# Attention ahead of two expert layers: exponentials transposed undivided, outputs multiplied by turned reciprocal sums

## The chip, the cores and the metric

The kernel runs on one core of a Trainium2 chip. [...] The metric is device time in microseconds; below are the median, the lowest and the highest of three runs.

## The reference

```python
def attention(q, k, v, M_prev, z_prev, beta):      # B, H, S, D = 4, 8, 576, 64
    scores = q @ k.T / 8, causal mask, minus the row's maximum
    a = np.exp(scores)
    a /= a.sum(-1, keepdims=True) + 1e-09
    local = a @ v
    q_p = phi(q)                                   # relu(x) + min(exp(x), 1)
    mem_out = (q_p @ M_prev) / (q_p @ z_prev + 1e-06)
    g = 1 / (1 + np.exp(-beta))                    # one per head
    return g * mem_out + (1 - g) * local

x = attention(...) as [2304, 512]
x = moe(x)      # gate by 8 rounds of row and column normalization; 8 experts 512 -> 1024 -> 512
return moe2(x)  # 512 -> 2048 -> 512, leaky relu
```

## The kernel before

Attention takes 32 heads in 16 pairs: a batch `b` and two neighbouring heads `j` = 0, 1. `run` (line 286) is a generator that emits the work of a pair and yields a number after each piece; what is emitted in between comes from outside. Up to the end of batch 0 the outside adds only the loading of weights. From then on, each yield adds one or two quarter steps of the first expert's products (`First.run`, tiles `ph`, `hh`, `hl`, `po`; 15 quarter steps in a pair). A planner then orders the instructions of each engine; where two are ready it keeps the order of emission. After the last pair come the gate, its normalization and the rest of the first expert, and from about 520 us on the other experts and the second layer, in an order written out by hand.

All products run on operands split in a high and a low part: ACT rounds the high part out of PSUM, DVE (or POOL) subtracts it from the source. So every transpose by PE (128x128 blocks against an identity) is followed by an ACT copy and a DVE subtraction.

A pair goes so. `load` (109) fetches q, k, v, M and z by DMA. `transposed` (127) turns q, k and, later, the features (`qT`, `kT`, `pT`; tile `tps`). `features` (158) makes phi(q) in place, multiplies by z, sums to `nrm`, and at line 177 POOL multiplies the features by g over the norm. For each head, `scores` (197) and `softmax` (208) work on five row blocks t: products into `sps`, a DVE instruction adds the mask and finds the maximum (214), an ACT exponential sums its row into `sm` (216). `normalize` (219) turns `sm` into (1 - g) over the sum and multiplies the blocks `a`: three on DVE (227), two on ACT (229). One head later, `turn` (235) transposes the blocks in three groups r, x, y into the `at_` tiles, of which there is one set. `outputs` (250) multiplies the turned features by M and the turned blocks by v, 18 products into one tile `avps`, and ACT copies half of it (270); `collect` (273) adds the other half on DVE (277). With the second head `collect` also rounds x to `xh` on DVE (280), stores x by DMA, and leaves `late`, by which POOL makes `xl` (282). `values` (179) splits v and M.

The head of index j is so emitted: scores and softmax of its blocks between the turns of the head before; `qT` of the next pair (j = 1); `outputs` of the head before, `normalize`, `collect` of the head before; then for j = 0 `values`, `late`, `pT`, `load` of the next pair, and for j = 1 `kT` and the first half of the features of the next pair. The tiles `sps`, `avps`, `tps` and the turned group y share the tag `big` in PSUM: three buffers in batch 0, two from then on.

Of the kernel before, what the change touches and what calls it, by code (L numbers as in the profile page):

```python
# [16 lines left out]
ALU = mybir.AluOpType  # L17
# [43 lines left out]
class Attention:  # L61
# [47 lines left out]
    def load(self, b, hp):  # L109
        nc, h0 = self.nc, 2 * hp  # L110
        r = {"b": b, "hp": hp}
        for nm, src in (("q", self.q), ("k", self.k), ("v", self.v)):
            t = self.nv if nm == "v" else self.sbt([P, 5, 2, D], "n" + nm)
# [44 lines left out]
    def features(self, r):  # L158
# [12 lines left out]
        nrm = self.sbt([P, 5, 2], "nrm")  # L171
# [4 lines left out]
        ph3 = ph.rearrange("p c h d -> p (c h) d")  # L176
        nc.gpsimd.tensor_mul(ph3, ph3, nrm.rearrange("p c h -> p (c h)").unsqueeze(2).to_broadcast([P, 10, D]))

# [14 lines left out]
    def head(self, r, j):  # L193
        sm, nm = self.sbt([P, 5], "sm", bufs=2), self.sbt([P, 5], "nm_", bufs=2)
        return {"r": r, "j": j, "a": {}, "sm": sm, "nm": nm}
# [23 lines left out]
    def normalize(self, s, t0, t1):  # L219
        nc, h = self.nc, 2 * s["r"]["hp"] + s["j"]  # L220
        sl = s["sm"][:, t0:t1]
        nc.vector.tensor_scalar(out=sl, in0=sl, scalar1=1e-9, scalar2=self.iomg[:, h:h + 1], op0=ALU.add, op1=ALU.mult)
        nc.vector.reciprocal(sl, sl)
        for t in range(t0, t1):
            a = s["a"][t]
            if t < 3:
                nc.vector.tensor_scalar(out=a, in0=a, scalar1=s["sm"][:, t:t + 1], scalar2=None, op0=ALU.mult)
            else:
                nc.scalar.activation(a, a, AF.Copy, scale=s["sm"][:, t:t + 1])  # L229
# [43 lines left out]
    def collect(self, s):  # L273
# [4 lines left out]
        if j == 1:  # L278
            hp, c0 = r["hp"], r["b"] * S
            nc.vector.tensor_copy(self.xh[:, hp, c0:c0 + S], r["x"])  # L280
# [5 lines left out]
    def run(self):  # L286
# [8 lines left out]
        for n in range(len(pairs)):  # L295
            last = n + 1 == len(pairs)
            for j in range(2):
                s = self.head(r, j)
                lo = self.turn(prev, "r") if prev is not None else None
# [28 lines left out]
                if j == 1 and not last:  # L328
                    self.transposed(nxt, "qT")
                if prev is not None:  # L330
                    self.outputs(prev)
                self.normalize(s, 0, 5)
                if prev is not None:
                    self.collect(prev)
                yield 4
                if j == 0:
                    self.values(r)
                    if prev is not None:
                        self.late()
                        if prev["r"]["hp"] == HP - 1:  # L340
                            yield ("done", prev["r"]["b"])
                    self.transposed(r, "pT")
                    if not last:
                        nxt = self.load(*pairs[n + 1])
                    yield 5
                elif not last:
# [831 lines left out]
```

## Time and profile before

| | |
|---|---|
| median of three runs | 2236.46 us (2235.49 to 2237.0) |
| profiled execution, first to last instruction | 2234.6 us |
| what the median has beyond that span | 1.9 us |
| PE busy | 2165.0 us (97%) |
| DVE busy | 1562.9 us (70%) |
| ACT busy | 870.0 us (39%) |
| POOL busy | 1108.8 us (50%) |
| attention, by the first and last rounding of x | 50.2 to 417.5 us |

Busy times are of the whole span, and their shares average over stages that have different limits. PE's durations overlap, since products are pipelined: a busy PE is not one at its peak.

### The profile page before, as it was taken

What the parts mean: (1) busy time and instruction counts of PE and PEld (TensorE: products, weight loads), DVE (VectorE), ACT (ScalarE), POOL (GpSimd) and SP (SyncE); (2) the same over time, 40 slices, a digit from 0 to 9 for tenths busy, and PEclk for the clock granted to TensorE, in tenths of its full rate; (3) what the DMA queues carried; (4) which work ended last, traced back from release to release, by engine and by line L of the source; (5) the groups of instructions that cost most, each with busy time, mean ns of one, the idle gap of its engine ahead of it and who ended that gap; (6) DMA issues with size and microseconds to landing.
All of it is one profiled execution on the core that took longest, in us unless ns stands there. A gap on an engine that the chain in (4) does not pass through costs nothing.

```text
span 2234.6 us, 36326 instructions
## 1 busy us (share of the span) xinstructions
PE 2165.0 (97%) x13973; PEld 1938.1 (87%) x13973; DVE 1562.9 (70%) x2904; ACT 870.0 (39%) x1753; POOL 1108.8 (50%) x993
## 2 busy tenths in 40 slices
PE   6799999989999999999999999999999999999999
PEld 5688889778888999998998988889898988898898
DVE  8989899565877777777777788855555554566565
ACT  7877777433332222223222233332333233332421
POOL 5132222244775455455444568854555543665550
PEclk9999999999999999999999999999999999999999
DMA  5233332224542222222124634421111152336111
GB/s 138 63 89 94 92 96 82 68 90 147 161 142 67 67 67 76 76 67 67 57 71 152 213 116 135 125 72 52 57 51 45 57 201 68 109 95 227 66 57 38
DMA packets 215757, 213.01 MB, mean 95 GB/s; under 512 B 71968, under 2 KB 169248, under 8 KB 214048
## 3 DMA queue, kind: packets, MB, share of 16 engines
q1 hardware_dynamic: 215584, 210.69, 30.4%
q8 instruction: 110, 1.80, 0.3%
q14 instruction: 63, 0.52, 0.1%
HBM read 157.83 MB, written 49.28 MB: 93 GB/s over the span
## 4 chain that ended last, share of the span: by engine, by line
PE 76%; DVE 9%; issue 5%; ACT 4%; POOL 4%; DMA 2%; SPq 0%; POOLq 0%; DVEq 0%; ACTq 0%
PE po L882 35%; PE pq L839 27%; PE pq L827 4%; PE ph L514 3%; PE po L522 2%; PE sps L206 2%; PE atps L245 1%; ACT a L229 1%; PE avps L261 1%; POOL stl L687 1%; DVE a L214 1%; ACT a L216 1%; DMA xa<-xd 1%; DVE x L277 1%; ACT x L270 0%
## 5 line engine op out<-in xcount | busy, mean ns | idle before, releaser
L882 PE MATMUL po<-w,hh 128*128 128x512 f32 x2592 | 810.6, 393 | 7.9 <-ACT acc L894 3.1
L882 PEld LDWEIGHTS po<-w,hh 128*128 128x128 f32 x2592 | 473.9, 188 | 106.2 <-DVE acc L892 3.3
L882 PE MATMUL po<-w,hl 128*128 128x512 f32 x1296 | 509.4, 393 | 0.0
L629 POOL TENSOR_TENSOR w0l<-raw,w0h 128x512 fp32r<-128x512 f32 x144 | 191.3, 1349 | 360.3 <-ACT w0h L628 360.3
L857 ACT ACTIVATE hh<-c 128x512 fp32r<-128x512 f32 x224 | 129.2, 624 | 476.0 <-DVE c L852 476.0
L882 PEld LDWEIGHTS po<-w,hl 128*128 128x128 f32 x1296 | 243.6, 188 | 56.1
L839 PE MATMUL pq<-Xh,w0h 128*128 128x256 f32 x960 | 266.2, 277 | 2.1 <-DVE uv L847 1.4
L839 PE MATMUL pq<-Xl,w0h 128*128 128x256 f32 x960 | 265.3, 276 | 0.0
L839 PE MATMUL pq<-Xh,w0l 128*128 128x256 f32 x960 | 265.1, 276 | 0.0
L858 DVE SCALAR_TENSOR_TENSOR hl<-c,hh 128x512 fp32r<-128x512 f32 x224 | 169.3, 797 | 79.3 <-ACT hh L857 79.3
L892 DVE SCALAR_TENSOR_TENSOR acc<-po,Pm,acc 128x512 f32<-128x512 f32 x252 | 178.4, 748 | 49.3 <-PE po L882 47.4
L629 POOL TENSOR_TENSOR w<-raw,w 128x512 fp32r<-128x512 f32 x144 | 199.8, 1405 | 1.7 <-ACT w L628 1.7
L847 DVE TENSOR_TENSOR uv<-pq,s 128x256 f32<-128x256 f32 x144 | 60.5, 420 | 191.8 <-ACT s L846 191.6
L839 PEld LDWEIGHTS pq<-Xh,w0h 128*128 128x128 f32 x960 | 180.1, 188 | 7.3 <-DVE uv L847 2.0
L839 PEld LDWEIGHTS pq<-Xl,w0h 128*128 128x128 f32 x960 | 180.2, 188 | 4.1
L839 PEld LDWEIGHTS pq<-Xh,w0l 128*128 128x128 f32 x960 | 180.2, 188 | 0.0
L846 ACT ACTIVATE s<-pq 128x256 f32<-128x256 f32 x144 | 54.9, 381 | 256.1 <-PE pq L839 256.0
L629 POOL TENSOR_TENSOR ql<-raw,qh 128x512 fp32r<-128x512 f32 x48 | 62.8, 1329 | 129.8 <-ACT qh L628 129.8
L861 ACT ACTIVATE hh<-c 128x512 fp32r<-128x512 f32 x64 | 40.5, 632 | 185.9 <-DVE c L860 185.9
L839 PE MATMUL pq<-Xh,w1h 128*128 128x256 f32 x384 | 106.1, 276 | 1.1 <-ACT xa L957 1.1
L839 PE MATMUL pq<-Xh,sh 128*128 128x256 f32 x384 | 106.0, 276 | 0.0
L839 PE MATMUL pq<-Xl,sh 128*128 128x256 f32 x384 | 106.0, 276 | 0.0
(325 smaller groups left out, 5557.4 us busy)
## 6 DMA issues: line engine op xcount, KB each, us to landing
raw<-in_moe_w_dram SPq DMA_DIRECT2D x136, 512.0 KB, 3.6
Xh<-kh SPq DMA_DIRECT2D x6, 1792.0 KB, 7.4
Xl<-kl SPq DMA_DIRECT2D x6, 1792.0 KB, 11.5
f<-in_moe_w_in_dram SPq DMA_DIRECT2D x16, 512.0 KB, 5.0
f<-in_moe_w_out_dram SPq DMA_DIRECT2D x16, 512.0 KB, 4.7
raw<-wide_in SPq DMA_DIRECT2D x16, 512.0 KB, 3.4
raw<-wide_out SPq DMA_DIRECT2D x16, 512.0 KB, 3.7
kh<-sth SPq DMA_DIRECT2D x12, 512.0 KB, 5.2
```

What stands on the lines that cost most here:

```text
L206: nc.tensor.matmul(ps[:, o_:o_ + kn], x[:, q0:q0 + P], y[:, k0:k0 + kn], start=(i == 0), stop=(i == len(terms) - 1))
L514: nc.tensor.matmul(ph[:, :T], wp[:, c, f0:f0 + P], x[:, c, t0:t0 + T], start=(n == 0), stop=(n == 11))
L522: nc.tensor.matmul(po, a[:, s], wp[:, c, :], start=(first and n == 0), stop=(last and n == 2))
L629: self.nc.gpsimd.tensor_sub(lo, src, f32(hi))
L827: nc.tensor.matmul(ph[:, f * SB:(f + 1) * SB], wp(a, c % 2), xp[x][:, c], start=(n == 0), stop=(n == 11))
L839: nc.tensor.matmul(b[-1][:, o:o + SB], wp(a, c), X[s][part][:, x, c], start=(n == 0), stop=(n == 5))
L846: nc.scalar.activation(s1, b[0][:, lo], AF.Copy)
L847: v.tensor_add(uv[:, 0], b[0][:, up], s1)
L857: nc.scalar.activation(hh[:, f], c, AF.Relu)
L858: v.scalar_tensor_tensor(out=hl[:, f], in0=c, scalar=0.0, in1=f32(hh[:, f]), op0=ALU.max, op1=ALU.subtract)
L882: nc.tensor.matmul(po[j], a[:, f, r], w[1, part][:, f], start=(fp == 0 and f == 0 and n == 0), stop=(fp == 1 and f == 1 and n == 2))
L892: nc.vector.scalar_tensor_tensor(out=acc[t], in0=po[j], scalar=Pm[:, t0 + t, e:e + 1], in1=acc[t], op0=ALU.mult, op1=ALU.add)
```

## The change

The exponentials are no longer divided. They are transposed as they are, and the output, which lies with the tokens along its columns, is multiplied at the end by a tile of reciprocal sums that has been turned in the same way. Since the features' part of the output is multiplied too, the features are first multiplied by the sums. The pair keeps both heads' sums in one tile `sm` of 5 by 2. The new `rows` (after the second head's softmax) makes sums / (1 - g), multiplies `nrm` by it, takes the reciprocals, has POOL multiply the features (the former line 177) and spread the reciprocals over 128 by 640. The new `spread` transposes that on PE into PSUM, and ACT copies it to `row`. `collect` has POOL multiply x by `row` and ACT, not DVE, round it. Since the features need both sums, `pT` moves to the end of the second head, and `outputs` of a pair's first head to the start of the next pair, ahead of the turns of the second head; those of the second head stay where they were, behind `spread`. q gets two buffers, and so does `nrm`. The last pair yields two more numbers.

```diff
-            t = self.nv if nm == "v" else self.sbt([P, 5, 2, D], "n" + nm)
+            t = self.nv if nm == "v" else self.sbt([P, 5, 2, D], "n" + nm, bufs=2 if nm == "q" else 1)
...
-        nrm = self.sbt([P, 5, 2], "nrm")
+        nrm = r["nrm"] = self.sbt([P, 5, 2], "nrm", bufs=2)
...
-        ph3 = ph.rearrange("p c h d -> p (c h) d")
+
+    def rows(self, r):
+
+        nc, h0 = self.nc, 2 * r["hp"]
+        sm, nrm = r["sm"], r["nrm"]
+        nc.vector.scalar_tensor_tensor(out=sm, in0=sm, scalar=1e-9, in1=self.iomg[:, h0:h0 + 2].unsqueeze(1).to_broadcast([P, 5, 2]),
+                                       op0=ALU.add, op1=ALU.mult)
+        nc.vector.tensor_mul(nrm, nrm, sm)
+        nc.vector.reciprocal(sm, sm)
+        ph3 = r["p"].rearrange("p c h d -> p (c h) d")
         nc.gpsimd.tensor_mul(ph3, ph3, nrm.rearrange("p c h -> p (c h)").unsqueeze(2).to_broadcast([P, 10, D]))
+        r["row"] = self.sbt([P, 5, 2, D], "rb")
+        nc.gpsimd.tensor_copy(r["row"].rearrange("p c h d -> p (c h) d"), sm.rearrange("p c h -> p (c h)").unsqueeze(2).to_broadcast([P, 10, D]))
...
-    def normalize(self, s, t0, t1):
-        nc, h = self.nc, 2 * s["r"]["hp"] + s["j"]
-        sl = s["sm"][:, t0:t1]
-        nc.vector.tensor_scalar(out=sl, in0=sl, scalar1=1e-9, scalar2=self.iomg[:, h:h + 1], op0=ALU.add, op1=ALU.mult)
-        nc.vector.reciprocal(sl, sl)
-        for t in range(t0, t1):
-            a = s["a"][t]
-            if t < 3:
-                nc.vector.tensor_scalar(out=a, in0=a, scalar1=s["sm"][:, t:t + 1], scalar2=None, op0=ALU.mult)
-            else:
-                nc.scalar.activation(a, a, AF.Copy, scale=s["sm"][:, t:t + 1])
+    def spread(self, r):
+
+        nc = self.nc
+        ps = self.big("rps")
+        for t in range(5):
+            q0 = 448 if t == 4 else t * P
+            nc.tensor.transpose(ps[:, P + q0:2 * P + q0], r["row"][:, t].rearrange("p h d -> p (h d)"), self.ident)
+        r["row"] = self.sbt([P, S], "row")
+        nc.scalar.activation(r["row"], ps[:, P:P + S], AF.Copy)
...
-            nc.vector.tensor_copy(self.xh[:, hp, c0:c0 + S], r["x"])
+            nc.gpsimd.tensor_mul(r["x"], r["x"], r["row"])
+            nc.scalar.activation(self.xh[:, hp, c0:c0 + S], r["x"], AF.Copy)
...
                 s = self.head(r, j)
+                if j == 0 and prev is not None:
+                    self.outputs(first)
+                    self.collect(first)
...
-                if j == 1 and not last:
-                    self.transposed(nxt, "qT")
-                if prev is not None:
+                if j == 1:
+                    self.rows(r)
+                    if not last:
+                        self.transposed(nxt, "qT")
+                elif prev is not None:
+                    self.spread(prev["r"])
                     self.outputs(prev)
-                self.normalize(s, 0, 5)
-                if prev is not None:
                     self.collect(prev)
...
-                    self.transposed(r, "pT")
+                    if not last:
+                        nxt = self.load(*pairs[n + 1])
+                    first = s
+                    yield 5
+                else:
                     if not last:
-                        nxt = self.load(*pairs[n + 1])
-                    yield 5
-                elif not last:
-                    self.transposed(nxt, "kT")
-                    yield 5
-                    f = self.features(nxt)
-                    next(f)
+                        self.transposed(nxt, "kT")
+                    yield 5
+                    self.transposed(r, "pT")
+                    if not last:
+                        f = self.features(nxt)
+                        next(f)
                     yield 6
...
+        self.outputs(first)
+        self.collect(first)
         for nm in "rxy":
             self.turn(prev, nm)()
             yield 7
+        self.spread(prev["r"])
         self.outputs(prev)
```

## Rows read from the trace of the kernel before

**Rows 1.** The page, busy time of each engine, share of the span, instructions:

```profile
PE 2165.0 (97%) x13973; PEld 1938.1 (87%) x13973; DVE 1562.9 (70%) x2904; ACT 870.0 (39%) x1753; POOL 1108.8 (50%) x993
```

**Rows 2.** Two lines' instructions: count, least/median/most ns, first and last start.

```profile
L280 DVE CAST xh<-x x16: 450/457/1030, 50.2 to 417.5; 128x576 fp32r<-128x576 f32 x16
...
L190 DVE TENSOR_TENSOR ms<-nm,ms x32: 196/222/1290, 14.7 to 395.2; 64x64 fp32r<-64x64 f32 x32
```

**Rows 3.** Windows: length, busy PE, PEld, DVE, ACT, POOL, clock, DMA, GB/s.

```profile
50.20:112.80 62.60, 49.06 (x329) 42.94 (x327) 58.61 (x165) 51.41 (x115) 13.89 (x13) 0.97 0.29 74
112.80:417.50 304.70, 295.39 (x2046) 265.23 (x2046) 271.07 (x698) 235.90 (x520) 84.53 (x70) 1.00 0.33 89
```

**Rows 4.** Late window by tile, in order: ph, po, atps, tps, avps, sps.

```profile
112.80:417.50 304.70, 82.72 (x540) 71.98 (x540) 18.70 (x45) 17.01 (x45) 1.00 0.33 89
...
112.80:417.50 304.70, 79.80 (x270) 46.44 (x270) 6.66 (x10) 0.00 (x0) 1.00 0.33 89
...
112.80:417.50 304.70, 49.73 (x357) 40.89 (x357) 52.11 (x72) 44.87 (x72) 1.00 0.33 89
...
112.80:417.50 304.70, 24.39 (x170) 19.26 (x170) 42.28 (x56) 36.26 (x56) 1.00 0.33 89
...
112.80:417.50 304.70, 61.34 (x432) 58.13 (x432) 18.13 (x25) 15.33 (x24) 1.00 0.33 89
...
112.80:417.50 304.70, 59.02 (x276) 41.11 (x276) 59.28 (x115) 1.00 0.33 89
```

**Rows 5.** PE's timeline, late stretch: start, duration; what follows gives the step.

```profile
239.20 0.28 PE L258 MATMUL avps<-pTh,ms 128*128 128x256 f32 x1
...
241.54 0.28 PE L514 MATMUL ph<-xh,w0h 128*128 128x256 f32 x1
...
242.24 0.71 PE L133 MATMUL tps<-ident,nq 128*128 128x128 f32 x5
242.71 0.36 PE L514 MATMUL ph<-xh,w0h 128*128 128x256 f32 x1
```

**Rows 6.** The chain that ended last, one late pair: start, duration, what.

```profile
241.28 1.39 ACT a L229 x2
...
244.18 0.61 DVE xh L280
```

**Rows 7.** DVE's groups to 430 us: busy us, mean ns, idle before.

```profile
L227 DVE TENSOR_SCALAR a<-a,sm 128x128 f32<-128x128 f32 (+2 forms) x96 | 29.8, 364 | 0.8
...
L222 DVE TENSOR_SCALAR sm<-sm,iomg 128x5 f32<-128x5 f32 x32 | 9.7, 304 | 4.1 <-ACT a L216 3.2
...
L223 DVE RECIPROCAL sm<-sm 128x5 f32<-128x5 f32 x32 | 6.1, 190 | 0.9
...
L173 DVE TENSOR_SCALAR nrm<-nrm 128x10 f32<-128x10 f32 x16 | 4.5, 279 | 0.0
```

**Rows 8.** ACT's groups to 430 us.

```profile
L229 ACT ACTIVATE a<-a,sm 128x512 f32<-128x512 f32 x64 | 45.2, 743 | 14.3 <-DVE sm L223 13.8
...
L150 ACT ACTIVATE pTh<-tps 128x576 fp32r<-128x576 f32 x16 | 10.4, 653 | 3.6 <-PE tps L133 3.2
```

**Rows 9.** The timeline of POOL and DVE around the fourth pair's rounding.

```profile
111.86 1.69 POOL L186 TENSOR_TENSOR vs<-nv,vs 128x320 fp32r<-128x320 f32 x2 [2.32 <-DVE vs L185]
...
112.84 1.03 DVE L280 CAST xh<-x 128x576 fp32r<-128x576 f32 x1
```

**Rows 10.** POOL's groups to 430 us.

```profile
L282 POOL TENSOR_TENSOR xl<-x,xh 128x576 fp32r<-128x576 f32 x16 | 22.9, 1432 | 20.8 <-DVE xh L280 20.8
L177 POOL TENSOR_TENSOR nq<-nq,nrm 128x640 f32<-128x640 f32 x16 | 20.2, 1262 | 147.1 <-PE sps L206 80.4 <-ACT a L216 40.3 <-ACT at_yh L247 17.1
...
L75 POOL MEMSET mask<- 128x640 f32 x1 | 0.6, 632 | 0.0
```

**Rows 11.** PE's groups to 430 us, the transposes of exponentials.

```profile
L245 PE MATMUL atps<-ident,a 128*128 128x128 f32 x480 | 67.9, 275 | 9.9 <-DVE a L227 5.3 <-ACT a L229 3.7 <-DVE nm__3497 L214 0.8
```

**Rows 12.** PE's timeline at the start, the first pair's feature transposes.

```profile
21.84 1.33 PE L133 MATMUL tps<-ident,nq 128*128 128x128 f32 x5 [4.71 <-POOL nq L177]
```

More of the change, by code (lines that the diff above doesn't have):

```diff
@@ L193, in head @@
     def head(self, r, j):
-        sm, nm = self.sbt([P, 5], "sm", bufs=2), self.sbt([P, 5], "nm_", bufs=2)
-        return {"r": r, "j": j, "a": {}, "sm": sm, "nm": nm}
+        if j == 0:
+            r["sm"] = self.sbt([P, 5, 2], "sm", bufs=2)
+        nm = self.sbt([P, 5], "nm_", bufs=2)
+        return {"r": r, "j": j, "a": {}, "sm": r["sm"][:, :, j], "nm": nm}
     def scores(self, s, t, ps, o):
```

## The prediction

> **What bounds the kernel now.** I read the page's busy line first: over the whole span PE is busy 97% [rows 1]. That is an average over stages, so I went to the stretches by windows, cut where line 280 ends a pair of heads. Its sixteen starts run from 50.2 to 417.5 us [rows 2], and the fourth, which closes batch 0, is at 112.84 [rows 9]. The change touches nothing after about 420 us.
>
> Early stretch, 50.2 to 112.8, three pairs of 20.9 us each: DVE is busy 58.6 of 62.6 us (94%), ACT 51.4 (82%), PE 49.1 (78%) [rows 3]. Attention runs alone here and DVE sets the pace.
>
> Late stretch, 112.8 to 417.5, twelve pairs of 25.4 us: the first expert's products fill PE. PE shows 295 busy of 305 us and DVE 271 (89%) [rows 3]. But PE's durations overlap, so I counted what it must at least issue. Six products of 256 columns take 0.70 us from start to start, 0.117 each; a pass of 18 output products takes 2.34; five transposes 0.47 [rows 5]. With the counts of [rows 4]: ph 540 x 0.117 = 63; po 270 of twice the columns, 0.234 each, 63; atps and tps 527 x 0.094 = 50; avps 432/18 x 2.34 = 56; sps 23 heads of 3968 columns (line 204) at 0.117 per 256, 42. Sum 274, so PE could have done this stretch in 90% of its time, with 31 us to spare. What eats those is the chain of waits: it passes through both divisions on ACT (1.39 us) and the rounding of line 280 (0.61) in one pair [rows 6].
>
> **The change part by part.** All prices are per pair.
>
> Removed. DVE: six multiplications of 0.364, two sums of 0.304, two reciprocals of 0.190, one rounding of 0.46 [rows 2, 7]: 2.18 + 0.61 + 0.38 + 0.46 = 3.6 us. ACT: four scalings of 0.743 in the mean = 3.0 us [rows 8].
>
> Added on DVE: two operations of 128x10, no dearer than the 0.279 of line 173, and a reciprocal of 0.19 [rows 7]: 0.75. DVE's net is -2.9.
>
> Added on ACT: the copy of the turned reciprocals out of PSUM is line 150's shape, 0.65; the rounding of x is between that and 0.74, the mean scaling [rows 8]; I take 0.74, since both read SBUF. Net -1.6.
>
> Added on PE: five transposes, 0.47 [rows 5], about 0.55 with the slower product behind them.
>
> Added on POOL: x times the turned row, 128x576, between nine tenths of line 177's 1.26 (1.14) and line 282's 1.43; I take 1.3. The broadcast copy lies between the 0.63 of a fill of that size and 1.26; I take 0.9 [rows 10]. Together 2.2, bounds 1.8 to 2.7. POOL is busy only 28% of the late stretch [rows 3].
>
> The added POOL time has a price on DVE. While POOL ran two subtractions from 111.86 to 113.55, the rounding on DVE that began at 112.84 took 1.03 us instead of 0.46 [rows 2, 9], and line 190's small subtraction takes 0.20 to 1.29 [rows 2]. Bounds: nothing, or all 2.2 us. I take 0.3, since most of DVE's work reads PSUM and shows no such spread. [...]
>
> Moved. The features' scaling now waits for both heads' sums, so pT stands behind a chain: small DVE work 0.55, POOL 1.26 [rows 10], PE 0.47 [rows 5], and the two halves of the split, which over the late stretch's 56 of them took ACT 36.3/56 = 0.65 and DVE 42.3/56 = 0.76 [rows 4]: 3.7 us. Behind the waiting transposes on PE stand the first head's output products, and behind those the next turns, whose at_ tiles they read. Cover: the next pair's q and k transposes with their copies, some 5 us of ACT and DVE work, and in the late stretch the fills. Without it the price is 3.7 per pair. ACT's rounding now waits for POOL's product (1.3, up to 2.7 behind another POOL operation); queued behind it are the next exponentials. DVE did that rounding without any wait. On SP the store of x waits for POOL too, with the next pair's loads behind it; they land half a pair before use, so I price this at nothing; uncovered it is the same 1.3. The second q buffer and doubled nrm cost nothing.
>
> Gone too: PE's waits for divided exponentials, 9.0 us over the stage [rows 11], and at the start the wait of 4.71 us for POOL's feature product [rows 12].
>
> The sum.
> - Start: of those 4.7 us I take 3; ACT's exponentials follow closely: -3.
> - Early, four pairs: DVE's floor at the same 94% would give -(2.9 - 0.3)/0.94 = -2.8, ACT's net alone -1.6. The two alternate on the chain, so the middle, -2.3: -9.
> - Late, twelve pairs: PE spares 31 - 12 x 0.55 = 24 us, 2.0 a pair. The chain loses more, but PE is not evenly loaded any more: both output passes (2 x 2.34) stand in the first half of a pair. I take a third, -0.7: -8.
> - End: the last pair has one more output pass before its turns, and POOL and ACT (2.0) before the gate's last operands, partly under the earlier gate blocks: +3 (0 to +6).
> Total -17. The profiled span is 2234.6, 1.9 us under the median of the runs, 2236.46, so 2217.6 in the span and 2219.5 as a median.
>
> **The rivals.**
> 1. Both floors are reached (early -2.8, late -2.0): -3 - 11 - 24 + 1 = -37, 2199. For it: the chain loses about 4 us a pair. Against: no pair of the late stretch has PE without waits.
> 2. POOL's 2.2 us go to DVE in full: DVE's net is -0.7 a pair, some -3 early; late nothing, where five transposes (+0.55 x 12 = 7 if PE-bound) eat what the start gave: 2233 to 2241, no change. For it: line 190's spread. Against: POOL's new work falls where DVE also reads PSUM. [...]
> 3. The halves of a late pair bind each for themselves, slower: the first is PE's (two passes 4.7, turns 15 x 0.094 = 1.4, scores 1.8, row 0.55, seven of a pair's fifteen fills, which are (63 + 63)/12 = 10.5, so 4.9: 13.3, at the 90% it reaches today 14.8), the second DVE's (by [rows 4] softmax 59.3/23 = 2.6, turns 52.1/24 = 2.2, q, k and pT 42.3/12 = 3.5, fills 18.7/12 x 8/15 = 0.8; small work 0.75; two feature passes of 640 columns, an estimate of 1.7 from the split's 0.76 for 576: 11.5, at 94% 12.3). 27.1 instead of 25.4 is +20 over twelve pairs; with start, early and end -9, that is +11, 2247. It decides from 0.75 us a pair on. Against: fills that are not ready slip into the second half by themselves, and softmax work runs ahead where PSUM lets it (two buffers of that kind, now with one more tile to pass through them).
> 4. The chain to pT stays uncovered: 16 x 3.7 = +59 against DVE's 42 (2.6 x 16) gives +17, 2254. It decides from 2.6 us a pair. For it: PE did wait 4.71 for this product at the start, when nothing else was ready.
>
> **How the numbers follow.** Forecast 0.58, rival 1 0.12, rival 2 0.13, rival 3 0.10, rival 4 0.07. About 4.5 us (0.2%) is what a measurement of this kernel tells from no change. Faster 0.70, same 0.13, slower 0.17. The range 2202 to 2246 leaves out most of rival 4 and the lowest part of rival 1, and spans the bounds of POOL's price and the uneven halves; the likeliest case's own range is 2207 to 2231.
>
> **What would show it.** Right: pair spacing near 18.6 us early and 24.7 late; DVE's share in the early stretch below 92% with ACT near 88%; the chain without any division and with q, k and feature work in its place; transposes of pT waiting for POOL under 1 us each. Wrong: late spacing at or over 25.4 with DVE idle in the first half (rival 3), PE waiting for line 177's successor over 2.6 us a pair (rival 4), or DVE operations of two SBUF inputs over a microsecond in every pair (rival 2).

## The result, and the profile after

Slower: 2268.74 us median of 4 runs (2267.43 to 2272.18), against 2236.73 (2235.49 to 2238.59) for the kernel before beside it; ratio 1.0145, 95% interval [1.0131, 1.0160]. The forecast was 2219.5 in a range of 2202 to 2246. What a run differs by from the kernel before on its own chip is given below as "+32.0 us" and the like; the intervals are 2 to 4 us to each side, so a difference of two runs is uncertain by 3 to 5.

The page of the kernel after, which answers to [rows 1]:

```profile
span 2267.9 us, 36478 instructions
...
PE 2189.6 (97%) x14053; PEld 1956.5 (86%) x14053; DVE 1525.9 (67%) x2776; ACT 849.4 (37%) x1721; POOL 1141.2 (50%) x1025
```

In this kernel PE runs the matrix products and the transposes, DVE and POOL the vector work and ACT the activations, each from a queue of its own; SP's queue issues the DMAs. DVE lost 37 us of work, ACT 21, and POOL gained 32: what was to move has moved. The span is 33.3 us longer all the same: PE is busy 24.6 us longer and idle 8.7 us longer (span less busy time: 78.3, before 69.6).

Line 292 is the rounding that line 280 was; its sixteen starts again cut the stretches, and line 291 is POOL's new product. The view is that of two lines: count, least/median/most ns, first and last start, and what the instruction's engine waited for ([rows 2]).

```profile
L291 POOL TENSOR_TENSOR x<-x,row x16: 1412/1430/1446, 48.1 to 451.6; 128x576 f32<-128x576 f32 x16
...
L292 ACT ACTIVATE xh<-x x16: 682/685/694, 49.5 to 453.0; 128x576 fp32r<-128x576 f32 x16
its engine sat idle before it (us, times) until:
  POOL x L291: 29.5, 16
```

The windows between the first, fourth and last of those starts answer to [rows 3]:

```profile
49.54:124.34 74.80, 57.63 (x340) 50.94 (x338) 53.50 (x136) 47.31 (x106) 20.36 (x18) 0.82 0.26 65
124.34:453.05 328.71, 307.93 (x2107) 272.85 (x2108) 242.56 (x602) 221.14 (x496) 107.93 (x94) 0.99 0.31 81
```

So the start gained 0.7 us, the three early spacings cost 12.2 (20.9 to 24.9 us a pair), the twelve late ones 24.0 (25.4 to 27.4) and what follows gained 2.2: +33.3 together. Of the 24.0, 6.1 are the first spacing, where the first expert begins and needs `xh` and `xl` at once (26.3 to 32.4), and 4.4 the last (18.6 to 23.0), which holds the end's extra output pass; the ten between them cost 1.35 each. Early, DVE's share fell from 94% to 72% and ACT's from 82% to 63%: the saved work became idle time. The clock fell from 0.97 to 0.82.

The turned row by windows (start, early, late; busy PE, weight load and ACT, clock, DMA), PE's transposes of the exponentials and POOL's groups to 453 us, which answer to [rows 4, 10, 11]:

```profile
0.00:49.50 49.50, 0.71 (x5) 0.58 (x5) 0.63 (x1) 0.93 0.54 138
49.50:124.30 74.80, 2.15 (x15) 1.65 (x15) 1.90 (x3) 0.82 0.26 65
124.30:453.00 328.70, 8.73 (x60) 6.50 (x60) 7.70 (x12) 0.99 0.31 81
```

```profile
L256 PE MATMUL atps<-ident,a 128*128 128x128 f32 x480 | 73.9, 278 | 11.7 <-ACT a L229 8.3 <-ACT hh L548 1.7 <-DVE at_rl L259 1.0
```

```profile
L291 POOL TENSOR_TENSOR x<-x,row 128x576 f32<-128x576 f32 x16 | 22.9, 1431 | 13.5 <-issue 13.5
...
L186 POOL TENSOR_TENSOR nq<-nq,nrm 128x640 f32<-128x640 f32 x16 | 20.7, 1293 | 50.4 <-DVE nrm L183 42.4 <-issue 8.0
L188 POOL COPY rb<-sm 128x640 f32<-128x640 f32 x16 | 12.7, 793 | 0.0
```

Five row transposes take PE 0.73 us a pair (8.73/12). POOL's prices came out near the forecast: 1.43 for the product (1.3), 0.79 for the copy (0.9).

One boundary of an early pair shows two of the new waits; it is the one with PE's longest wait for POOL. POOL, PE and ACT in the timeline (start, duration, what, idle before and what ended it):

```profile
80.35 1.77 POOL L186 TENSOR_TENSOR nq<-nq,nrm 128x640 f32<-128x640 f32 x1 [4.90 <-DVE nrm L183]
...
81.04 1.76 DVE L169 TENSOR_TENSOR ex<-nq,nz 128x640 f32<-128x640 f32 x1
...
82.17 1.33 PE L133 MATMUL tps<-ident,nq 128*128 128x128 f32 x5 [2.93 <-POOL nq L186]
...
83.54 0.65 ACT L150 ACTIVATE pTh<-tps 128x576 fp32r<-128x576 f32 x1 [3.70 <-PE tps L133]
...
84.24 0.58 PE L269 MATMUL avps<-pTh,ms 128*128 128x256 f32 x1 [0.74 <-ACT pTh L150]
...
84.62 0.63 PE L219 MATMUL sps<-k,qh 128*128 128x256 f32 x2
...
88.03 0.41 PE L272 MATMUL avps<-at_xh,vs 128*128 128x256 f32 x1
```

PE's next scores at 84.62 need nothing of `pT`, but stand in PE's queue behind its transposes, which wait 2.93 us for POOL. The windows of 5 us from 75 on show PE's clock beside its idle time:

```profile
75.00:80.00 5.00, 2.13 (x16) 1.42 (x14) 3.88 (x7) 4.78 (x11) 0.45 (x1) 0.97 0.32 73
80.00:85.00 5.00, 2.09 (x8) 1.69 (x9) 4.38 (x7) 0.65 (x1) 3.03 (x2) 0.50 0.04 9
85.00:90.00 5.00, 5.00 (x24) 5.00 (x23) 2.59 (x11) 2.70 (x7) 0.00 (x0) 0.51 0.34 75
```

PE is busy 43% and 42% in the first two; in the second the granted clock is 0.50, in the third, in which PE is busy throughout, 0.51, and the first head's output products of 256 columns take 0.41 us where such products took 0.28 in the late stretch of before ([rows 5]), at a clock of 1.00.

Where the waits are, over 0 to 125 us and then 125 to 430 (us in total, times, longest; the rounding at 124.34 is in both lists):

```profile
PE atps L256 <- ACT a L229: 8.3, 10, 2.2
...
ACT xh L292 <- POOL x L291: 7.1, 4, 2.4
...
PE tps L133 <- POOL nq L186: 5.9, 4, 2.9
```

```profile
ACT x L281 <- PE avps L272: 24.0, 20, 2.0
ACT xh L292 <- POOL x L291: 20.8, 11, 2.5
ACT at_rh L258 <- PE avps L272: 15.2, 9, 2.6
```

In all, ACT waits 29.5 us for POOL's new product, once in each of the 16 pairs. PE's four waits for the features in the first list are 1.25 us at the start, then 0.63, 2.93 and 1.09 at the three early boundaries; its transposes of exponentials still wait 8.3 us for ACT, though nothing is divided any more.

### The profile page after: what moved, and what is told of

It reads as the page before. It is cut to its first block, busy times and chain, and to the rows that moved or that the text cites. A ratio compares the mean times of both kernels' runs of the same rounds, so it can differ in the third digit from the quotient of the medians.

```text
span 2267.9 us, 36478 instructions
## 1 busy us (share of the span) xinstructions
PE 2189.6 (97%) x14053; PEld 1956.5 (86%) x14053; DVE 1525.9 (67%) x2776; ACT 849.4 (37%) x1721; POOL 1141.2 (50%) x1025
## 4 chain that ended last, share of the span: by engine, by line
PE 72%; DVE 9%; POOL 7%; ACT 5%; issue 5%; DMA 2%; SPq 0%; DVEq 0%; POOLq 0%; ACTq 0%
PE po L904 33%; PE pq L861 25%; PE pq L849 3%; PE avps L272 2%; PE ph L536 2%; PE po L544 2%; ACT a L229 2%; PE sps L219 1%; PE atps L256 1%; DMA raw<-in_moe_w_dram 1%; PE avps L269 1%; POOL x L291 1%; POOL stl L709 1%; POOL w0l L651 1%; DVE hl L880 1%
## 5 line engine op out<-in xcount | busy, mean ns | idle before, releaser
L197 POOL TENSOR_TENSOR vs<-nv,vs 128x320 fp32r<-128x320 f32 x32 | 27.4, 877 | 163.3 <-DVE vs L196 163.3
```

## The experiments

Three theories came out of that trace. Theory 1: the wait at the pair's boundary (`pT` behind POOL's product of the features, ahead of the next scores). Theory 2: the new order itself, with both output passes in one half of a pair. Theory 3: ACT's rounding waits for POOL's product of the outputs, with the next exponentials queued behind it. Theory 4, on what the saving can give back at all, came with e9.

### The order and the arithmetic apart: e1, e2

e1 is the kernel before with the moves alone: the division stays, and so does the cast on DVE.

```diff
-            t = self.nv if nm == "v" else self.sbt([P, 5, 2, D], "n" + nm)
+            t = self.nv if nm == "v" else self.sbt([P, 5, 2, D], "n" + nm, bufs=2 if nm == "q" else 1)
...
+                if j == 0 and prev is not None:
+                    self.outputs(first)
+                    self.collect(first)
...
-                if prev is not None:
+                if j == 0 and prev is not None:
                     self.outputs(prev)
...
                     yield 5
+                    self.transposed(r, "pT")        # was behind values and late of j = 0
```

> The kernel before with the order of the change alone: pT at the end of the second head, the first head's outputs at the start of the next pair, q in two buffers; the exponentials are still divided, the features are multiplied half a pair earlier by the norm alone, x is rounded on DVE. Theory 1 (the wait at the pair's boundary: pT's transposes stand in PE's queue behind POOL's product, which needs both heads' sums, and ahead of the next scores): that wait is gone here, so 2232 to 2243, pairs at 20.5 to 21.5 us early and 25 to 26 late, PE's clock as before. Theory 2 (the order itself: two output passes in one half of a pair): most of the 32 us stays, 2258 to 2268, late pairs near 27.

Measured: 2253.38 us, +17.3, ratio 1.0071 [1.0055, 1.0088]; early spacing 22.6, late 26.6, switch to the first expert 31.3. The time lies between the two expectations and meets neither. Half of the loss needs no new arithmetic.

e2 is the kernel after in the old order. It leaves out the features' multiplication by the sums, which the old place of `pT` doesn't allow.

```diff
-        nc.vector.tensor_mul(nrm, nrm, sm)
...
-        nc.gpsimd.tensor_mul(ph3, ph3, nrm...)      # in rows; back in features, as before
...
-                if j == 0 and prev is not None:
-                    self.outputs(first)
```

> The changed kernel in the old order: exponentials undivided, x multiplied by the turned row on POOL and rounded on ACT, but pT and the first head's outputs where they were. It leaves out the features' multiplication by the sums, so the memory part of the output is divided by sums it was not multiplied by; instructions, shapes and engines are those of the change. Theories 1 and 2: DVE's saving comes through, 2215 to 2228, early pairs at 18.5 to 19.5 us. Theory 3 (ACT, waiting for POOL's x with the next exponentials behind it, 1.7 us a pair): no faster than before, 2236 to 2262, with ACT's wait for POOL still 25 to 30 us in all.

Measured: 2242.24 us, +6.1, ratio 1.0027 [1.0017, 1.0037]. That is in theory 3's range, with ACT's wait for POOL at 25.4 us. Early DVE fell to 78% busy and the spacing rose to 22.0. ACT, DVE and POOL of e2 show why (timeline, one early pair):

```profile
69.64 1.44 POOL L290 TENSOR_TENSOR x<-x,row 128x576 f32<-128x576 f32 x1
```

```profile
69.68 0.28 DVE L226 CUSTOM_DVE_ANT_0 a<-sps,mask 128x128 f32<-128x128 f32 x1
69.89 0.08 DVE L226 DVE_READ_ACCUMULATOR2_ANT nm__791<- 128x1 f32 x1
...
73.40 0.96 DVE L258 TENSOR_TENSOR at_yl<-atps,at_yh 128x768 fp32r<-128x768 f32 x1 [1.40 <-ACT at_yh L257]
```

```profile
69.29 0.60 ACT L257 ACTIVATE at_xh<-atps 128x512 fp32r<-128x512 f32 x1 [0.42 <-PE atps L255]
71.11 0.69 ACT L291 ACTIVATE xh<-x 128x576 fp32r<-128x576 f32 x1 [1.22 <-POOL x L290]
71.70 0.39 ACT L228 ACTIVATE a<-a,nm__791 128x128 f32<-128x128 f32 x1
```

The first exponential's maximum is there at 69.97 and the exponential starts at 71.70: ACT sits idle for 1.22 us with that work ready behind the rounding, then rounds. DVE, with less to do, waits for ACT in turn.

### The boundary: e3, e4

e3 adds 32 products without use before `pT`'s transposes in batch 0, to test whether PE's clock then stays up.

```diff
+WARM = 32
...
+        self.zero = self.sb.tile([P, 256], F32R, name="zero")
+        nc.vector.memset(f32(self.zero), 0.0)
...
+        if nm == "pT" and r["b"] == 0:
+            for _ in range(WARM):
+                nc.tensor.matmul(ps[:, 768:1024], self.zero[:, :P], self.zero, start=True, stop=True)
```

> The changed kernel with 32 throwaway products of 256 columns (zeros, into unused columns of the same PSUM tile) ahead of pT's transposes in batch 0, about 3.7 us of PE work at each of four boundaries, where PE otherwise waits. If the clock's fall after the boundary is a cost of its own: the clock stays near 1.0 from 50 to 125 us, early pairs fall from 24.9 to about 22 us, total 2256 to 2262. If the clock's fall only accompanies the wait: no gain, 2268 to 2276.

Measured: 2266.57 us, +30.5, ratio 1.0135 [1.0120, 1.0150]. The clock over the early stretch is 0.98 and its spacing 23.0 instead of 24.9, but the late spacing stays at 27.5. By this trace the fall of the clock is a cost of about 2 us per early pair; the time is only 1.5 us better than the changed kernel's, meets neither expectation, and its interval overlaps that kernel's. The clock is a small part of the whole.

e4 puts `pT`'s transposes and the first head's pass, and with them the turn r behind that pass, behind the next pair's first two blocks of scores.

```diff
-                if j == 0 and prev is not None:
-                    self.outputs(first)
-                    self.collect(first)
...
                 self.softmax(s, 1, ps, 512)
+                if j == 0 and prev is not None:
+                    self.transposed(prev["r"], "pT")
+                    self.outputs(first)
+                    self.collect(first)
```

> The changed kernel with pT's transposes and the first head's outputs moved behind the next pair's first two score blocks, so that PE can make these scores while POOL multiplies the features. Theory 1: scores no longer wait, early pairs 21 to 22.5 us, late pairs 25.3 to 26.3, total 2240 to 2252. Theories 2 and 3: within 5 us of the changed kernel, 2264 to 2273.

Measured: 2272.75 us, +36.7, ratio 1.0165 [1.0150, 1.0180]. That mend returns nothing, as theories 2 and 3 expected, and theory 1 as a theory of the whole falls.

### POOL's two products: e5, e6, e7

```diff
-            nc.gpsimd.tensor_mul(r["x"], r["x"], r["row"])
+            nc.vector.tensor_mul(r["x"], r["x"], r["row"])
```

e5 is the kernel after with that line alone; e6 is e2 with it (with e2's omission); e7 is e5 with the product of line 186 on DVE too.

> The changed kernel with the product of the outputs and the turned reciprocal row on DVE instead of POOL; nothing else. Theory 3 (ACT's rounding waits for POOL's 1.41 to 1.45 us product, with the next exponentials queued behind it): the wait of 20.8 us over 11 late pairs and 7.1 us over 4 early ones goes, DVE pays about 0.8 us a pair, the late spacing falls from 27.4 to about 26.4 us, the switch to the first expert from 32.4 to about 30 us, the time to 2248 to 2256 us. Theory 1 (pT behind POOL's other product, the one of the features, at the pair's boundary): unmoved, early spacing stays above 24 us, 2264 to 2272 us. Theory 2 (two output passes in one half): the gain stops at what the order alone costs, about 2253 us.

> The arithmetic alone in the old order (as in the run that measured 2242; the features are not multiplied by the sums, which is left out) with the outputs' product by the row on DVE instead of POOL. Theory 3: the arithmetic's saving was there and was given back by ACT's wait for POOL; early spacing falls from 22.0 to about 20 us, the late one from 25.9 to about 25 us, the time to 2222 to 2232 us. Rival (the arithmetic relieves engines that set nothing: DVE was 80% busy in the early stretch and the spacing did not fall; the order in which PE's transposes stand sets the pace): 2236 to 2244 us with DVE still under 85% busy early.

> The changed kernel with both of POOL's products of a pair (outputs by row, features by sums) on DVE; POOL keeps the copy of the reciprocals. Theory 1: PE's wait before pT's transposes (2.9 us in early pairs) shrinks to about 1.5 us, TensorE's clock stays near full in 50 to 113, early spacing about 22 to 23 us, 6 to 12 us under the kernel with only the outputs' product on DVE. Theory 3 alone: no more than 2 us under that kernel. Theory 2: both stop at about 2253 us, the price of the order.

Measured: e5 2248.90 us, +12.7, ratio 1.0058 [1.0043, 1.0073]; e6 2234.32, -1.9, 0.9991 [0.9981, 1.0000]; e7 2244.15, +8.0, 1.0038 [1.0023, 1.0053]. DVE's prices in e7 (mean ns) are below POOL's for both:

```profile
L186 DVE TENSOR_TENSOR nq<-nq,nrm 128x640 f32<-128x640 f32 x16 | 12.2, 764 | 0.0
...
L291 DVE TENSOR_TENSOR x<-x,row 128x576 f32<-128x576 f32 x16 | 16.3, 1020 | 0.1
```

The windows of e5 and e7 between the same starts, early and late, and ACT's wait in e5:

```profile
48.26:113.28 65.02, 53.38 (x343) 46.96 (x344) 55.42 (x141) 46.48 (x104) 15.12 (x15) 0.92 0.29 73
113.28:429.86 316.58, 302.93 (x2107) 272.21 (x2106) 254.45 (x616) 221.21 (x495) 91.34 (x82) 1.00 0.32 85
```

```profile
46.35:114.08 67.73, 56.87 (x352) 49.86 (x351) 58.15 (x145) 47.15 (x106) 13.77 (x13) 0.87 0.29 74
114.08:429.02 314.94, 303.78 (x2107) 271.64 (x2106) 262.30 (x628) 221.03 (x496) 80.95 (x70) 1.00 0.32 85
```

```profile
L292 ACT ACTIVATE xh<-x x16: 683/686/688, 48.3 to 429.9; 128x576 fp32r<-128x576 f32 x16
its engine sat idle before it (us, times) until:
  DVE x L291: 14.1, 15
```

One product taken out of ACT's way returns 19.3 us of the 32.0 (e5), and 8.0 us in the old order (e2 to e6): theory 3 holds and is the largest single cost. ACT's wait before the rounding falls from 29.5 us to 14.1. The early spacing falls from 24.9 to 21.7 us, that is 9.8 of the 12.2 lost there, with the clock at 0.92; theory 1 had expected it to stay above 24, since the features' product is still POOL's, and PE's early waits for that are still there (1.09, 1.20 and 1.19 us). So the early loss too hangs mostly on POOL's product of the outputs.

The features' product is worth 4.7 more (e5 to e7), just clear of the noise of two runs, and between theory 1's 6 to 12 and theory 3's 2 or less. It does not come from the early boundary: there the spacing rises again, to 22.6 us with the clock at 0.87. By the traces, the start is 1.9 us shorter, the early stretch 2.7 longer, the late one 1.6 shorter, and 3.9 are gained after the last rounding, where no edit changes anything and where the traces of this case differ by up to 5.9 us. So its cause is open.

In the old order (e6) the change comes out 1.9 us ahead, which is within what can't be told from no change, though it still leaves work out. That misses both expectations of e6: theory 3's 2222 to 2232 by 2.3 us and the rival's 2236 to 2244 by 1.7, with the early spacing at 20.8 (from 22.0), the late one at 25.4, and DVE 87% busy where the rival wanted under 85%.

### What the division is worth: e9, e10

e9 is the kernel before without the five multiplications of `a` per head, with nothing in their place; it leaves out the division.

```diff
-        for t in range(t0, t1):
-            a = s["a"][t]
-            if t < 3:
-                nc.vector.tensor_scalar(out=a, in0=a, scalar1=s["sm"][:, t:t + 1], ...)
-            else:
-                nc.scalar.activation(a, a, AF.Copy, scale=s["sm"][:, t:t + 1])
```

> The kernel before without the in-place scaling of the exponentials (three operations of DVE and two of ACT per head; the sums and their reciprocals are still formed). It leaves out the division, and adds nothing in its place. Theory of the prediction (the scaling on DVE and ACT paces both stretches): early spacing falls from 20.9 to 18.6 us or less, late from 25.4 to 24.7 us or less, the time to 2217 us or less. Theory 4 (late, TensorE is the bound at 295.4 of 304.7 us busy, so only what is left of its idle time can come back; early, no engine's sum but the order of the queues sets the pace): late spacing not under 25.0 us, early not under 19.8 us, the time 2228 to 2235 us.

Measured: 2224.22 us, -13.6, ratio 0.9939 [0.9922, 0.9955]. Between the two: theory 4 expected 2228 to 2235, the prediction's reading 2217 or less. The windows of e9:

```profile
47.59:105.58 57.99, 49.07 (x331) 43.23 (x329) 53.19 (x148) 43.95 (x102) 12.46 (x12) 0.97 0.31 80
105.58:405.05 299.47, 293.60 (x2040) 264.19 (x2040) 254.37 (x626) 207.13 (x472) 83.87 (x70) 1.00 0.34 91
```

Early a pair gains 1.5 us (20.9 to 19.3) and DVE is still at 92%; late it gains 0.4 (25.4 to 25.0) with PE at 98%. So the early stretch does follow the scalings' work, and the late one hardly any; e9 takes DVE's and ACT's share away together, so it doesn't tell which of the two paces the early pairs.

e10 is the kernel before with the row's copy, its five transposes and ACT's copy added and not used (the copy reads the features' reciprocals, which are there earlier, and stands ahead of the features' product in POOL's queue).

```diff
+        nc.gpsimd.tensor_copy(r["row"].rearrange(...), nrm...to_broadcast([P, 10, D]))
...
                 if prev is not None:
+                    if j == 0:
+                        self.spread(prev["r"])
                     self.outputs(prev)
```

> The kernel before with the turned row added and not used: POOL's copy of a pair's reciprocals (here those of the features, formed earlier), five transposes on TensorE, one ACT copy a pair; everything else stays. Theory 4 (TensorE is the bound late): the 60 transposes of the late stretch, 8.7 us in the changed kernel's rows, come out one to one, with ACT's copy on top where an early pair waits; 2244 to 2250 us, late spacing 26.1 us or more. The prediction's costing (the transposes lie in TensorE's gaps): 2234 to 2239 us.

Measured: 2243.05 us, +5.2, ratio 1.0022 [1.0012, 1.0033]; early spacing 22.1, late 25.6. A miss for both: the cost is there, but it falls first on the early pairs (1.2 us each, 3.7 in all), and late, where theory 4 put it, only 0.2 a pair of PE's 0.73 comes out (2.3 in all). In its early stretch PE has a wait (us in total, times, longest) that the kernel before doesn't have:

```profile
PE avps L270 <- ACT row L241: 2.2, 3, 0.8
```

In each early pair the output pass behind the row's transposes waits for ACT's copy of the row. Nothing in e10 reads that copy; what the two share is the tag `big`, so the pass waits for the PSUM buffer that the copy sets free.

### What is left of the order: e8, e16, e11 to e15, e17, e18

e8 and e16 are the same kernel: e1's move of the first pass alone, `pT` staying in the first half; e16 is for its trace.

```diff
 # against e1
                 if j == 0:
                     self.values(r)
                     ...
+                    self.transposed(r, "pT")
...
-                    self.transposed(r, "pT")
```

> The kernel before (divided, features' product where it was) with one thing moved: the first head's output pass into the next pair's first half; pT's transposes stay in the middle of the pair. Theory 2 (two output passes in one half upset the order): about 2250 us, late spacing 26.3 to 26.8 us, as with both moves. Theory 1 (what costs is that pT stands at the pair's boundary ahead of the next scores): 2234 to 2241 us, late spacing 25.3 to 25.7 us, early spacing 21 us.

> The first head's output pass moved alone, a second time, for its trace: 2238 to 2241 us; late spacing 25.3 to 25.8 us by theory 1, 26 us or more by theory 2.

Measured: 2239.80 us, +3.6, ratio 1.0015 [1.0006, 1.0025], and 2239.45, +4.4, 1.0019 [1.0008, 1.0029]; spacings of e16 21.1 and 25.8. Two passes in one half are cheap; `pT`'s move, with the second q buffer that came with it, is some 13 of e1's 17. Of the 4.8 us that e16's late spacings cost, 3.0 are the first one, at the switch (29.3).

e17 is e8's kernel with the second q buffer, which nothing in it needs.

```diff
-            t = self.nv if nm == "v" else self.sbt([P, 5, 2, D], "n" + nm)
+            t = self.nv if nm == "v" else self.sbt([P, 5, 2, D], "n" + nm, bufs=2 if nm == "q" else 1)
```

> The first head's output pass moved alone (2239.5), plus the second buffer for q that the moved pT needs, and that nothing here needs. If what the move of pT costs (13 us) is the buffer (other addresses for all later tiles, earlier loads): 2248 to 2254 us. If it is the move itself: 2236 to 2242 us.

Measured: 2244.41 us, +7.1, ratio 1.0033 [1.0021, 1.0046]: between the two expectations, and its interval overlaps e16's. By the medians the buffer is up to 3 or 4 of the 13, not all.

e13 is e1 with `pT`'s transposes in the middle of the second half; e14 is e1 with each pass's two `pT` products behind those of the turned exponentials instead of ahead.

```diff
 # e13 against e1
-                    self.transposed(r, "pT")
...
+                if j == 1:
+                    self.transposed(r, "pT")
                 lo = self.turn(prev, "y") if prev is not None else None
 # e14 against e1, in outputs' group
-            for i, p in enumerate(r["pT"]):
-                nc.tensor.matmul(..., start=(i == 0), stop=False)
             for i, (c, nm, s0, sn) in enumerate(parts):
                 ...
+            for i, p in enumerate(r["pT"]):
+                nc.tensor.matmul(..., start=False, stop=(i == 1))
```

> The kernel before with the new order of the output passes, as in the run of the order alone (2253), but pT's transposes stand in the middle of the pair's second half, ahead of the third block of turned exponentials, instead of at the pair's boundary. Theory 1 (what the order costs is pT's place at the boundary, where q, k and pT are all turned and moved out of PSUM one after the other): 2237 to 2243 us, that is what moving the first pass alone cost, late spacing under 26 us. Theory 2 (two passes in one half): 2249 to 2256 us.

> The order alone (2253), with each output pass's two products with pT at the end of their group instead of the start, so that at the boundary TensorE can run the turned exponentials' products while pT is moved out of PSUM. If TensorE's wait for pT's movement is what the boundary costs (3.0 us over 2 early pairs in the order-alone trace): 2243 to 2248 us. If the cluster of movements on ACT and DVE costs it, or two passes in one half do: 2250 to 2256 us.

Measured: e13 2252.71 us, +17.6, ratio 1.0076 [1.0060, 1.0093]; e14 2251.38, +16.3, 1.0074 [1.0059, 1.0089]. Both bring the early spacing back from 22.6 to 21.2, near the 20.9 of before, and both lose it late: 26.9 and 26.7 (e1 26.6). Both times are in the ranges of theory 2, e14's also in that of the movements on ACT and DVE. Windows of e1 and of e13:

```profile
50.73:118.66 67.93, 53.87 (x333) 47.01 (x331) 61.70 (x166) 53.16 (x115) 13.72 (x13) 0.90 0.29 71
118.66:437.70 319.04, 301.76 (x2058) 268.15 (x2058) 276.12 (x698) 238.55 (x518) 83.41 (x69) 1.00 0.32 84
```

```profile
49.43:112.99 63.56, 49.41 (x326) 42.21 (x324) 59.96 (x162) 52.48 (x113) 12.72 (x13) 0.97 0.28 69
112.99:435.69 322.70, 299.66 (x2058) 267.83 (x2058) 277.07 (x698) 238.22 (x519) 83.93 (x70) 1.00 0.31 83
```

The wait for `pT` at the boundary is thus most of the early part of the order's cost (e13's early stretch is 4.4 us shorter), and not the late part: e13's PE is idle late for 23.0 us where e1's is for 17.3.

e12 and e15 are e7 with e4's and e14's edits; e11 is e7 with the second head's pass (and `spread`, `values`, `late` and the next loads) moved to the start of the second half; e18 is e7 with the first expert's steps dealt 4 to the half with both passes and 11 to the other, instead of 7 and 8.

```diff
 # e11 against e7
+                elif j == 1:
+                    if second is not None:
+                        self.spread(second["r"])
+                        self.outputs(second)
+                        self.collect(second)
+                    self.values(r)
 # e18 against e7; the yields of j = 1 are numbered 11 to 16
-FILL = {1: 1, 2: 2, 3: 2, 4: 1, 5: 1, 6: 1, 7: 2}
+FILL = {1: 0, 2: 1, 3: 1, 4: 1, 5: 1, 11: 2, 12: 3, 13: 3, 14: 1, 15: 1, 16: 1, 7: 2}
```

> The changed kernel with both products of a pair on DVE, and the second head's output pass moved from the end of the next pair's first half to the start of its second half, so that each half holds one pass (the values' split and the next loads follow it). Theory 2 (two passes in one half upset the order): 4 us or more under the kernel with both products on DVE, 2236 to 2241 us. Theory 1 (pT at the pair's boundary, ahead of the next scores, is what is left): unmoved, 2242 to 2247 us.

> The changed kernel with both products of a pair on DVE, and pT's transposes and the first head's output pass behind the next pair's first two blocks of scores. Theory 1 (the boundary): TensorE has scores to run while DVE forms the features' product, early spacing about 21 us with the clock near full, 2234 to 2240 us. Rival (the same work in the same half, only in other places of the queue): within 4 us of the kernel with both products on DVE, 2241 to 2249 us.

> The changed kernel with both products of a pair on DVE (2244), with the pT products at the end of their groups. If TensorE's wait for pT's movement is what is left (3.4 us over 3 early pairs there): 2236 to 2241 us. If not: 2242 to 2247 us.

> The changed kernel with both products of a pair on DVE (2244), and the first expert's steps dealt out by half: 4 in the half that holds both output passes (7 before), 11 in the other (8 before), the total as it was. Theory 2 in a narrower form (late, both passes stand in one half while the fill of TensorE by the first expert is dealt out evenly, so that TensorE is overfull in one half and waits in the other): late spacing from 26.3 to 25.5 us, 2232 to 2239 us. If the fill is not what the order upsets: 2242 to 2250 us.

Measured: e11 2245.78 us, +7.9, ratio 1.0040 [1.0025, 1.0055]; e12 2256.79, +18.9, 1.0090 [1.0075, 1.0105]; e15 2259.30, +24.2, 1.0109 [1.0094, 1.0124]; e18 2245.71, +8.4, 1.0038 [1.0023, 1.0053]. None returns anything of e7's +8.0, and e12 and e15 add 11 and 16 to it, which neither of their expectations allowed. Evening out the passes or the fill is not what is missing: theory 2 falls in its narrower form (e18), and as a theory of two passes in one half it has e8, e11 and e16 against it and only the times of e13 and e14 for it. Theory 1's mends cost more than they mend.

Settled: the sizes of the division, of the row and of POOL's product of the outputs, and that the order costs most of its early part at the boundary. Open: what the 4.7 us of the features' product consist of, and why the late stretch takes about 1 us a pair more in the new order, some 8 to 14 us in all. Part of that is at its ends: of e1's 14.3 late us, 5.0 are the switch and 1.5 the last spacing. Every edit of the order also changes what the planner puts ahead of what on every engine, and no run here holds all but one of these still. No version that computes the reference beat the kernel before, and no run points to one.

## Why the prediction was wrong

What failed is the step "Moved": it named the waits and priced them, but put nothing for them into the sum. For `pT` it named a cover; for ACT's rounding behind POOL's product (1.3 us, the next exponentials behind it) it gave none, and this term, put at nothing without a reason, measured 19.3 us. By the prediction's own steps:

- **Removed, and the forecast's floor.** Right in kind, near in size. The scalings alone are worth 13.6 us (e9). "DVE sets the pace" early agrees, though ACT's work went with it: DVE's 2.18 us less a pair give 1.5. Late, "the chain loses more, I take a third" gave -0.7 a pair for the whole change; the scalings alone give 0.4. PE's waits for divided exponentials, 9.0 us and called gone, came back as waits for the exponentials themselves, 8.3 us (line 256).
- **Added on PE.** Costed at 0.55 a pair and hidden. PE's time was 0.73 and the row costs 5.2 us (e10), 1.2 us in each early pair, where PE had seemed to have room (49 of 62.6 us busy); each of them has a wait of PE of 0.74 to 0.76 for ACT's copy of the row, which the prediction didn't have.
- **Added on POOL.** The durations were right (1.43 and 0.79), and what POOL's new work cost DVE is small: line 169, which took 1.76 beside POOL's product at 81.04, has a median of 0.82, and DVE's net came to -37 us over 16 pairs where 2.9 a pair is -46, which leaves it some 9 us by that count. In e5, too, DVE's busy time over the early and late stretches rises by 13.8 us for 15 products of 1.04 (mean): what POOL no longer does gave DVE back some 1.8 us by that count. In the trace of before, as the prediction had it, most of DVE's work up to 430 us reads PSUM (253 of 374 us) and shows no spread like line 190's: line 277 took 749 to 761 ns in its 32 sums, line 142 741 to 764. Rival 2's price on DVE is there in single rows and, with DVE idle for 28% of the early stretch, doesn't make the time.
- **ACT's rounding behind POOL's product.** The prediction wrote that "queued behind it are the next exponentials" and that DVE did this rounding without any wait, and carried it at nothing. It is the largest term: 29.5 us of ACT's waiting over 16 pairs, 19.3 us of time (e5 against after).
- **The chain to `pT`.** Priced at 3.7 uncovered and taken as covered by the next pair's q and k transposes and, late, by the fills. PE waited for POOL's product 0.63, 2.93 and 1.09 us at the three early boundaries, 4.7 in all, and its clock fell near each, to 0.50, 0.50 and 0.62 in windows of 5 us from 55, 80 and 110: early, that cover held for a part of the chain, not for all. Moving the product to DVE gives 4.7 us back, not in these pairs (e5 to e7). Late it mostly is covered, as forecast: POOL's product held PE only twice after 124 us, for 1.6 us together.
- **Start and end.** Of the -3 at the start 0.7 came: PE's wait of 4.71 ([rows 12]) went, but `xh` now waits for POOL's 1.43. The end was forecast at +3; its extra pass and POOL's and ACT's work stand ahead of the last rounding, and that last spacing grew by 4.4, while what follows it gained 2.2.

Of the rivals, 3 named the late size best (27.1 us a pair, measured 27.4, with DVE idle), but its reason, uneven halves, did not survive e11 and e18. Rival 4's wait for the product is real early and is far from its 3.7 a pair throughout. No rival joined the two waits for POOL to the cost of the order: 19.3 (product in ACT's way) + 4.7 (features' product) + 9.9 (e6 to e7: the order, with the features multiplied by the sums and their product on DVE) - 1.9 (arithmetic in the old order, e6) = 32.0. The sum is a path through four kernels, so it gives the loss whatever the terms are: the first product is worth 8.0 in the old order, so the terms are not independent of each other.

Even without the waits little was to be had: of the division's 13.6 us the row takes 5.2, and in e6, which pays for the product on DVE as well (1.0 us a pair), 1.9 are left; no run parts the rest.

## What to carry to other kernels

Work taken off a busy engine is worth what the next wait lets through: list each new wait with what stands behind it in its engine's queue, and put its full price into the sum unless a row shows the cover. An off-path engine's product is cheap as busy time and dear once an engine on the path waits for it with other work queued behind: here one 1.4 us product a pair on POOL, between DVE's sum and ACT's rounding, cost 19.3 us, where the whole division is worth 13.6; in the old order it cost 8.0. A new tile in a shared set of buffers is such a wait too (e10: 2.2 us of PE's time over three early pairs). When a change bundles an arithmetic and an order, run them apart first; here either alone was a loss as written.

## What the runs showed of the hardware

- The features' product of 128x640, whose second operand is a broadcast of 128x10, took DVE 761 to 766 ns in all 16 pairs of e7, and POOL 1262 (median, after). In each of these pairs POOL's copy of 128x640 ran beside it; DVE's time hardly varied, and the copy took 1100 ns (median) instead of the 719 of the kernel after.
- The outputs' product of 128x576 by a full tile took POOL 1430 ns (after) and DVE 748 to 1340, median 1070 (e7). The twelve that met POOL's subtraction for `vs` (line 197, two SBUF operands) for 0.39 us or more took 1004 to 1340, the four that met it for 0.14 us or less 748 to 759.

```profile
L291 DVE TENSOR_TENSOR x<-x,row x16: 748/1070/1340, 45.6 to 428.2; 128x576 f32<-128x576 f32 x16
L188 POOL COPY rb<-sm x16: 1096/1100/1112, 26.7 to 413.8; 128x640 f32<-128x640 f32 x16
```

- When POOL and DVE each ran a product of two SBUF operands of 128x640 at once (after, at 80.35 and 81.04), they took 1.77 and 1.76 us; the medians of the two lines are 1.26 and 0.82.
- Around the boundary at 82 us of the kernel after, PE was idle for 1.52 us (ACT) and then 2.93 (POOL); the granted clock fell to 0.50 within the second wait and was 0.51 over 85 to 90, in which PE was busy throughout. With products without use in front of such boundaries the early stretch had 0.98 for 0.82 (e3).
